# A long convolution by Fourier transforms in front of a feed-forward layer: the transform over s2 split by halves instead of parities

## The chip, the core and the metric

The kernel runs on one core of a Trainium2 chip. The metric is the device time of one execution in microseconds. A ratio is the mean time of one kernel's runs over the mean of the kernel before's runs of the same rounds. A kernel counts as faster or slower only beyond 2%.

A few words that the text uses. A *stage* is a stretch of the execution with one kind of work. A *group* is the work on one pair of frequencies k1, of which there are 45 for each of the four batches. The *period* of batch 0's groups is the length of their stage divided by 44. The *tail* is the stretch after the last group's filter product in which the remaining steps of batch 0 run out, before the feed-forward layer starts.

## The reference

```python
def _attn_ref(x, v, pos_emb, w1, w2):          # x, v: (4, 12544, 128)
    h_mlp = np.maximum(pos_emb @ w1, 0.0) @ w2
    h_filt = h_mlp * np.exp(-0.01 * pos)[:, None]
    u = x * v
    Uf = np.fft.rfft(u, n=2 * S, axis=1)
    Hf = np.fft.rfft(h_filt, n=2 * S, axis=0)
    y = np.fft.irfft(Uf * Hf[None], n=2 * S, axis=1)[:, :S, :]
    return x * y

def _moe_ref(x, w1, w2, w3, w_out):            # x: (50176, 128), d_ff 768
    h = np.maximum(np.maximum(x @ w1, x @ w2), x @ w3)
    return h @ w_out
# output: _moe_ref(_attn_ref(...).reshape(50176, 128), ...)
```

The kernel makes the convolution from matmuls with tables of sines and cosines. A position is n*128 + s2. The first transform runs over n and leaves, for every s2, 90 frequencies k1. The second runs over s2 and leaves the frequencies k2. Then comes the product with the filter's transform. The third transform goes back to s2 and the last one back to n.

## The kernel before

The 128-point transform over s2 is never done whole. Before the change it is split by the parity r of s2: each parity is transformed alone, and the sum and difference of the two results (a butterfly) give the lower and the upper half of k2. After the product, another sum and difference (`g_unfold`, whose result is `ab`) prepares the two inputs of the third transform. The cuts from the code leave out lines that only name or rearrange views (`v`, `xt`, `d0` and the like); other gaps are marked with three dots.

```python
def first_halves(ps, lhs, table, dst, copy):        # first transform, then one copy
    for i, a in enumerate(lhs):
        for r in range(2):
            for c in range(2):
                nc.tensor.matmul(ps[64 * c:64 * c + 64, 256 * i + r * N1:256 * i + (r + 1) * N1],
                                 a[:, r, :], table[:, c * N1:(c + 1) * N1], ...)
    copy(dst, ps[:].rearrange("p (s m) -> p s m", m=256)[:, :, 0:2 * N1].rearrange(
        "p s (r k) -> p k r s", r=2))

def evens(ps, eo):                                  # ScalarE
    nc.scalar.copy(eo[:], v[:, :, 1, :])
def butterfly(ps, eo, xs):                          # VectorE, from PSUM
    nc.vector.tensor_tensor(out=xs[:, :, 0, :], in0=eo[:], in1=v[:, :, 0, :], op=ALU.add)
    nc.vector.tensor_tensor(out=xs[:, :, 1, :], in0=eo[:], in1=v[:, :, 0, :], op=ALU.subtract)
def g_re(g):                                        # product: both inputs in SBUF
    nc.vector.tensor_tensor(out=xt[:], in0=xt[:], in1=hts[g][:, 0], op=ALU.mult)
def g_im(g):
    nc.vector.tensor_tensor(out=xss[g][:], in0=xss[g][:], in1=hts.pop(g)[:, 1], op=ALU.mult)
def g_sum(g, eng):
    eng.tensor_tensor(out=xts[g][:], in0=xts[g][:], in1=xss.pop(g)[:], op=ALU.add)
def g_unfold(g):                                    # both inputs in SBUF
    for q, op in enumerate((ALU.add, ALU.subtract)):
        nc.vector.tensor_tensor(out=ab[:, :, q, :], in0=y[:, :, 0, :], in1=y[:, :, 1, :], op=op)
def g_third(b, g): ...                              # third transform of ab
def g_pair(g):                                      # batches 1 to 3: from PSUM
    nc.vector.tensor_tensor(out=zs[:, a], in0=ps[:, 0:256], in1=z1[:], op=op)

# ... beside the feed-forward layer: the slots of one group (a slot is some 2.9 us)
            at(s, 1, g_second, g)
            at(s + 1, 0, g_butterfly, g)
            at(s + 2, 1, g_swap, g)
            at(s + 3, 0, g_re, g)
            at(s + 4, 0, g_im, g)
            at(s + 5, 0, g_sum, g, nc.gpsimd)
            at(s + 7, 0, g_unfold, g)
            at(s + 8, 1, g_third, b, g)
            at(s + 9, 0, g_pair, g)
            at(s + 10, 0, g_store, b, g, nc.gpsimd)

# ... one hidden block of the feed-forward layer
        halves_mm(pa[:, 0:N], w_sb[1][:, f * P:(f + 1) * P], rhs, True, True)
        nc.scalar.activation(h[:], pa[:, 0:N], Relu)
        halves_mm(pb[:, 0:N], w_sb[2][:, f * P:(f + 1) * P], rhs, True, True)
        nc.vector.tensor_tensor(out=h[:], in0=h[:], in1=pb[:, 0:N], op=ALU.max)
```

Batch 0 is transformed alone, before the feed-forward layer starts; batches 1 to 3 are transformed beside the feed-forward layer of the batch before them.

## Time and profile before

The median of four runs is 2479.1 us (2478.58 to 2484.12). I cut the profiled execution at five events: the data's first transform, the first and the last product that makes the filter (`sps`), and the first matmul of the last transform (`yps`), where the feed-forward layer starts.

| stage of the kernel before | from, us | to, us | length, us |
|---|---|---|---|
| set-up, filter's network and first transforms | 0 | 67.1 | 67.1 |
| first transforms of batch 0 | 67.1 | 127.1 | 60.0 |
| 45 groups of batch 0, a period of 4.02 us | 127.1 | 303.8 | 176.7 |
| tail | 303.8 | 320.4 | 16.6 |
| four feed-forward stages | 320.4 | 2480.6 | 2160.2 |

The view by windows of the kernel before shows four of these stages. The columns are window, length, busy us of PE, PEld, DVE, ACT and POOL with their instructions, granted clock, DMA share and GB/s.

```profile
67.10:127.10 60.00, 59.09 (x1190) 54.70 (x1188) 30.97 (x73) 40.39 (x50) 1.54 (x2) 1.00 0.74 173
127.10:303.80 176.70, 175.82 (x2458) 146.13 (x2456) 155.05 (x313) 151.96 (x268) 46.23 (x88) 1.00 0.88 267
320.40:897.50 577.10, 547.29 (x6344) 378.57 (x6346) 395.34 (x739) 222.87 (x454) 354.21 (x390) 0.99 0.75 177
897.50:1474.80 577.30, 545.61 (x6628) 371.77 (x6626) 425.12 (x761) 230.06 (x468) 370.42 (x411) 0.99 0.78 183
```

Take the first row. TensorE is busy for 59.09 of 60 us, and GpSimd does nothing (1.54 us): the first transforms are bound by TensorE. In the second row TensorE has 175.82 of 176.7. The two feed-forward rows leave 30 and 32 us of TensorE idle each. That idle time is what the change wants.

### The profile page before, as it was taken

How to read it: one execution, taken by the hardware profiler on the slowest of the kernel's cores; microseconds unless marked ns; L12 is line 12 of the kernel's file. 1: busy time of each engine (PE TensorE's matmuls, PEld its weight loads, DVE VectorE, ACT ScalarE, POOL GpSimd, SP SyncE). 2: the span in 40 equal slices, each digit the busy share in tenths (PEclk: the TensorE clock that was granted, in tenths of full speed). 3: DMA queues.
4: the chain of work that ended last, by engine and by line, in shares of the span. 5: the costliest groups of instructions: out<-in, count | busy, mean ns of one | idle time of the engine just before them, and what ended most of it. 6: DMA issues, size and time to landing. Idle time of an engine off the chain costs nothing.

```text
span 2480.6 us, 70451 instructions
## 1 busy us (share of the span) xinstructions
PE 2373.3 (96%) x29025; PEld 1655.7 (67%) x29025; DVE 1628.5 (66%) x3044; ACT 1008.8 (41%) x1981; POOL 1395.9 (56%) x1595
## 2 busy tenths in 40 slices
PE   9999999999999899999999999998999999999999
PEld 8988867766666656666666666765666666666665
DVE  4588847577777756667888856758878873333333
ACT  2688834444334324434434433443444432222222
POOL 1022247566656567646666667656666665555565
PEclk9999999999999999999999999999999999999999
DMA  6879889777677649958778749967787843222231
GB/s 147 193 237 275 265 163 187 144 189 213 170 197 203 156 112 200 183 132 215 201 200 212 208 120 176 189 149 197 193 214 193 216 125 90 51 67 60 54 73 21
DMA packets 459275, 408.67 MB, mean 165 GB/s; under 512 B 322660, under 2 KB 338333, under 8 KB 458953
## 3 DMA queue, kind: packets, MB, share of 16 engines
q1 hardware_dynamic: 417664, 315.23, 54.2%
q0 software_dynamic: 28464, 75.72, 11.1%
q10 hardware_dynamic: 12825, 13.21, 1.7%
q8 instruction: 228, 3.74, 0.6%
q14 instruction: 94, 0.77, 0.1%
HBM read 295.76 MB, written 84.67 MB: 153 GB/s over the span
## 4 chain that ended last, share of the span: by engine, by line
PE 81%; DVE 11%; DMA 4%; issue 2%; ACT 1%; SPq 0%; ACTq 0%; POOL 0%; DVEq 0%; POOLq 0%
PE pb L131 17%; PE pa L131 17%; PE ops L624 17%; PE ps L131 12%; PE ps L140 7%; PE yps L131 5%; DVE ab L444 4%; PE sps L798 3%; DMA ht<-hd 3%; DVE hid L578 2%; DVE zs L470 1%; DVE xs L434 1%; PE pm L304 1%; PE gps L784 1%; DVE xt L431 1%
## 5 line engine op out<-in xcount | busy, mean ns | idle before, releaser
L578 DVE TENSOR_TENSOR hid<-hid,pb 128x392 f32<-128x392 f32 x768 | 429.1, 559 | 506.6 <-PE pb L131 439.6
L575 ACT ACTIVATE hid<-pa 128x392 f32<-128x392 f32 x768 | 382.3, 498 | 709.3 <-PE pa L131 682.7
L131 PE MATMUL pa<-gt,w_sb 128*64 128x392 f32 x3072 | 641.0, 495 | 0.0
L131 PE MATMUL pb<-gt,w_sb 128*64 128x392 f32 x3072 | 638.6, 494 | 0.6 <-ACT hid L575 0.6
L131 PEld LDWEIGHTS pb<-gt,w_sb 128*64 128x64 f32 x3072 | 221.2, 137 | 288.8 <-issue 271.6
L624 PE MATMUL ops<-hid,wo_sb 128*64 128x196 f32 x3072 | 330.9, 329 | 0.0
L624 PEld LDWEIGHTS ops<-hid,wo_sb 128*64 128x64 f32 x3072 | 220.6, 137 | 138.3 <-issue 113.0
L649 POOL DMA_DIRECT2D out_dram<-o x256 | 162.7, 640 | 264.4 <-DVE o L644 104.8
L131 PE MATMUL ps<-ab,wt 128*64 128x128 f32 x2880 | 205.5, 281 | 87.2 <-DVE ab L444 84.4
L594 POOL TENSOR_TENSOR s<-hid 128x392 f32<-128x392 f32 x192 | 205.2, 1069 | 134.0 <-DVE hid L578 130.9
L594 POOL TENSOR_TENSOR s<-hid,s 128x392 f32<-128x392 f32 x192 | 200.7, 1045 | 97.7 <-DVE hid L578 96.8
L444 DVE TENSOR_TENSOR ab<-xt 128x256 f32<-128x256 f32 x360 | 252.5, 741 | 1.6
L131 PEld LDWEIGHTS ps<-ab,wt 128*64 128x64 f32 x2880 | 162.1, 138 | 130.8 <-DVE ab L444 110.6
L594 POOL TENSOR_TENSOR hid<-hid,s 128x392 f32<-128x392 f32 x192 | 206.4, 1081 | 42.6 <-DVE hid L578 24.4
L437 POOL TENSOR_TENSOR xt<-xt,xs 128x512 f32<-128x512 f32 x135 | 172.4, 1277 | 96.5 <-DVE xs L434 81.6
L131 PEld LDWEIGHTS pa<-gt,w_sb 128*64 128x64 f32 x3072 | 200.7, 138 | 20.1 <-issue 2.2
L431 DVE TENSOR_TENSOR xt<-xt,ht 128x512 f32<-128x512 f32 x180 | 203.0, 1128 | 13.9 <-ACT ht L803 13.7
L594 POOL TENSOR_TENSOR hid<-hid 128x392 f32<-128x392 f32 x192 | 209.8, 1111 | 0.2
L131 PE MATMUL ps<-spec,wt 128*64 128x128 f32 x2880 | 189.2, 273 | 2.1 <-issue 2.1
L140 PE MATMUL ps<-f,uT 98*64 98x90 f32 x4096 | 188.1, 241 | 2.4 <-ACT spec L144 2.3
L140 PEld LDWEIGHTS ps<-f,uT 98*64 98x64 f32 x4096 | 176.4, 137 | 12.2 <-ACT spec L144 5.5
L624 PE MATMUL ops<-s,tw 128*64 128x196 f32 x1536 | 171.3, 329 | 0.0
(105 smaller groups left out, 3083.4 us busy)
## 6 DMA issues: line engine op xcount, KB each, us to landing
wt<-wt_const SPq DMA_DIRECT2D x360, 256.0 KB, 4.7
ht<-hd SPq DMA_DIRECT2D x270, 256.0 KB, 4.4
zd<-zs POOLq DMA_DIRECT2D x135, 256.0 KB, 3.6
zt<-zd SPq DMA_DIRECT2D x192, 180.0 KB, 4.3
ut<-in_xr_dram SPq DMA_DIRECT2D x128, 196.0 KB, 4.1
ut<-in_vr_dram SPq DMA_DIRECT2D x128, 196.0 KB, 4.2
xT<-in_x_dram SPq DMA_DIRECT2D x256, 98.0 KB, 4.2
out_dram<-o POOLq DMA_DIRECT2D x256, 98.0 KB, 3.3
```

Of the source, the lines that this page charges most:

```text
L131: nc.tensor.matmul(out[64 * h:64 * h + 64], lhsT[:, 64 * h:64 * h + 64], rhs, start=start, stop=stop, skip_group_check=True)
L140: nc.tensor.matmul(ps[64 * c:64 * c + 64, 256 * i + r * N1:256 * i + (r + 1) * N1], a[:, r, :], table[:, c * N1:(c + 1) * N1], start=(i % ...
L304: nc.tensor.matmul(ps[64 * h:64 * h + HH, 512 * r + q * FO:512 * r + (q + 1) * FO], posv[64 * h:64 * h + 64, P - 1 - 2 * (8 * i + q) - r, ...
L431: nc.vector.tensor_tensor(out=xt[:], in0=xt[:], in1=hts[g][:, 0], op=ALU.mult)
L437: eng.tensor_tensor(out=xts[g][:], in0=xts[g][:], in1=xss.pop(g)[:], op=ALU.add)
L444: nc.vector.tensor_tensor(out=ab[:, :, q, :], in0=y[:, :, 0, :], in1=y[:, :, 1, :], op=op)
L575: nc.scalar.activation(h[:], pa[:, 0:N], Relu)
L578: nc.vector.tensor_tensor(out=h[:], in0=h[:], in1=pb[:, 0:N], op=ALU.max)
L594: nc.gpsimd.tensor_tensor(out=out[:], in0=a[:], in1=b[:], op=op)
L624: nc.tensor.matmul(ps[64 * c:64 * c + 64, 0:H2], w, rhs[:, :, c, :], start=start, stop=True, skip_group_check=True)
L649: nc.gpsimd.dma_start(dst[64 * m:64 * m + 64, 4 * i + c:4 * i + 8:2, b, :], t[m][64 * c:64 * c + 64].rearrange("d k (q n) -> d (k q) n", q=2))
L798: nc.tensor.matmul(ps[64 * h:64 * h + 64, (2 * c + k) * 2 * D:(2 * c + k + 1) * 2 * D], G[:, k, c], w2x[:].rearrange("p s d -> p (s d)"), ...
```

## The change

The transform over s2 is split by the halves w of s2 instead. The two halves are summed and subtracted straight after the first transform, while they lie in first-stage PSUM (`over_w`); each result is then transformed to one parity c of k2. There is no butterfly after the second transform, so the product can read the second transform from PSUM, and no sum stands between the product and the third transform. On the way back the two parities are summed out of third-stage PSUM (`g_over_c`), one half is turned by a quarter (`g_turn`), and `g_pair` joins the two k1. In batch 0, some of the new half-sums go to GpSimd (`over_w_there`, `filter_over_w`). The filter's product becomes 32 matmuls of 64 rows in quarters of the array, in place of 16 of 128 rows. Batch 0's last transform takes the half-size table that the other batches already had.

```diff
+    def over_w(ps, dst, tmp):
+        v = by_r(ps)                                # "p (s m) -> p s r k"
+        nc.scalar.copy(tmp, v[:, :, 1, :])
+        for c, op in enumerate((ALU.add, ALU.subtract)):
+            nc.vector.tensor_tensor(out=dst[:, :, c, :].rearrange("p k s -> p s k"), in0=tmp,
+                                    in1=v[:, :, 0, :], op=op)
+    def over_w_there(ps, dst, tmp):
+        nc.scalar.copy(tmp, v[:, :, 1, :])
+        nc.scalar.copy(d0, v[:, :, 0, :])
+        nc.gpsimd.tensor_tensor(out=d1, in0=tmp, in1=d0, op=ALU.subtract)
+        nc.gpsimd.tensor_tensor(out=d0, in0=tmp, in1=d0, op=ALU.add)
+    def as_it_is(ps, dst):
+        nc.scalar.copy(dst.rearrange("p k r s -> p s r k"), by_r(ps))
...
     def g_re(g):
-        nc.vector.tensor_tensor(out=xt[:], in0=xt[:], in1=hts[g][:, 0], op=ALU.mult)
+        nc.vector.tensor_tensor(out=xt[...], in0=ps[:], in1=hts[g][:, 0]..., op=ALU.mult)
-    def g_unfold(g): ...
+    def g_over_c(g):                                # VectorE, from PSUM
+        dt = state["cv"][0].tile([P, 5, D], FP32, tag="dt", name="dt", bufs=1)
+        for w, op in enumerate((ALU.add, ALU.subtract)):
+            nc.vector.tensor_tensor(out=dt[...], in0=c0, in1=c1[:], op=op)
+    def g_turn(g):                                  # ScalarE
+        nc.scalar.copy(dt[0:64, 3, :], dt[64:128, 4, :])
+        nc.scalar.mul(dt[64:128, 3, :], dt[0:64, 4, :], -1.0)
     def g_pair(g):                                  # now both inputs in SBUF, all batches
-            nc.vector.tensor_tensor(out=zs[:, a], in0=ps[:, 0:256], in1=z1[:], op=op)
+            nc.vector.tensor_tensor(out=zs[:, a], in0=dt[:, 0:2, :], in1=dt[:, 2:4, :], op=op)
...
+            at(s + 1, 0, g_swap, g)
+            at(s + 1, 0, g_re, g)
+            at(s + 2, 0, g_im, g)
+            at(s + 3, 0, g_sum, g)
+            at(s + 5, 1, g_third, g)
+            at(s + 6, 0, g_over_c, g)
+            at(s + 6, 1, g_turn, g)
+            at(s + 7, 1, g_pair, g)
+            at(s + 9, 0, g_store, b, g)
...
+    def filter_over_w(k):                           # the filter's half-sums, five k at a time
+        nc.gpsimd.tensor_tensor(out=t, in0=s1, in1=s0, op=ALU.subtract)
+        nc.gpsimd.tensor_tensor(out=s0, in0=s1, in1=s0, op=ALU.add)
+        nc.scalar.copy(s1, t)
...
             quad([t[:, 4 * v + i] for i in range(4)], f1[:], spec[:, :, :, at:at + 4],
+                 over_w_there if (u + v) % 5 in (1, 3) else over_w)
+            if at < 4 * N1 // 5:
+                filter_over_w(5 * at // 4)
...
+    for s in range(-1, NK + 5):                     # batch 0's groups
+        s_filter(s); g_second(s); g_swap(s); g_re(s)
+        s_second(s + 1)
+        g_turn(s - 3)
+        g_third(s - 2)
+        g_im(s); g_sum(s)
+        g_pair(s - 3)
+        g_over_c(s - 2)
+        g_store(0, s - 4)
...
-                        G[:, k, c], w2x[:].rearrange("p s d -> p (s d)"), start=(k == 0),
+                            G[64 * c:64 * c + 64, k, ri, :], w2x[64 * c:64 * c + 64],
```

The loop over batch 0's groups is shown without its conditions on s, and its weight loads are left out.

## The prediction

> **What bounds the kernel now.** I read the page's busy times and chain first, to see which engine carries the time.
>
> ```profile
> PE 2373.3 (96%) x29025; PEld 1655.7 (67%) x29025; DVE 1628.5 (66%) x3044; ACT 1008.8 (41%) x1981; POOL 1395.9 (56%) x1595
> ...
> PE 81%; DVE 11%; DMA 4%; issue 2%; ACT 1%; SPq 0%; ACTq 0%; POOL 0%; DVEq 0%; POOLq 0%
> ```
>
> TensorE is busy for 96%, but 11% of the chain is VectorE. So the bulk is matmul time that this change leaves alone, and the prize is in the stretches where VectorE ends the wait. I then cut the span into stages with the view by windows. Set-up and first transforms run to 124 us; batch 0's middle transform with the filter (45 groups) to 304; then four feed-forward stages, the first three of which carry the next batch's transform: inputs and first transform first, then 45 groups of second transform, product and third transform. Four of the windows inside the feed-forward stages:
>
> ```profile
> 506.00:885.00 379.00, 351.30 (x3953) 241.94 (x3950) 280.55 (x535) 148.58 (x309) 237.83 (x248) 0.99 0.69 180
> 910.00:1080.00 170.00, 168.13 (x2312) 116.57 (x2310) 108.29 (x189) 69.18 (x133) 114.73 (x144) 1.00 0.97 179
> 1085.00:1460.00 375.00, 345.18 (x3994) 234.59 (x3992) 303.77 (x544) 151.60 (x316) 238.84 (x248) 0.99 0.71 188
> ...
> 1660.00:2035.00 375.00, 345.48 (x3998) 235.00 (x3995) 303.45 (x548) 152.44 (x317) 238.78 (x248) 0.99 0.71 189
> ```
>
> Columns: window, length, busy us of PE, PEld, DVE, ACT, POOL, clock, DMA share, GB/s. Where first transforms are made (910 to 1080) TensorE idles 2 us of 170. Where the groups run it idles 28, 30 and 30 us, 87 in all, with VectorE 74 to 81% busy. The waits from 325 to 2030 us say for what:
>
> ```profile
> PEld ps L131 <- DVE ab L444: 105.6, 73, 4.9
> ...
> PE ps L131 <- DVE ab L444: 83.9, 64, 4.6
> ```
>
> `ab` is the sum and difference of the product, made by VectorE just before the third transform. 64 waits, 84 us: practically all of the idle time. Why VectorE is late shows in the groups of lines of 1085 to 1460 us:
>
> ```profile
> L444 DVE TENSOR_TENSOR ab<-xt 128x256 f32<-128x256 f32 x90 | 76.2, 885 | 0.0
> ...
> L431 DVE TENSOR_TENSOR xt<-xt,ht 128x512 f32<-128x512 f32 x45 | 61.4, 1365 | 0.0
> L434 DVE TENSOR_TENSOR xs<-xs,ht 128x512 f32<-128x512 f32 x45 | 34.7, 771 | 0.0
> L470 DVE TENSOR_TENSOR zs<-ps,z 128x256 f32<-128x256 f32 x88 | 32.9, 415 | 0.0
> ```
>
> The same forms in 124 to 304 us, where GpSimd only issues transfers:
>
> ```profile
> L444 DVE TENSOR_TENSOR ab<-xt 128x256 f32<-128x256 f32 x86 | 32.7, 422 | 1.5
> ...
> L431 DVE TENSOR_TENSOR xt<-xt,ht 128x512 f32<-128x512 f32 x44 | 30.4, 691 | 13.6 <-ACT ht L803 13.3
> ```
>
> 885 against 422 ns, 1365 against 691 ns: beside GpSimd's arithmetic, the operations with both inputs in SBUF take twice their time. The one with an input in PSUM (`zs`) stays at 415.
>
> **What the skill says.** The Trainium skill, "SBUF — State Buffer", section "SBUF: two separate sides": GpSimd and a VectorE operation with two SBUF inputs take a shared port pair as an exclusive lock for a whole instruction. The trace agrees (the pairs above; the longest `ab` took 4.86 us). "PSUM — Partial Sum Buffer", "The four PSUM rules": GpSimd cannot touch PSUM; so whatever this change reads from PSUM it must leave to VectorE or ScalarE. "TensorEngine Tiling (Array Packing)", "Key Properties": 64x64 tiles work independently, and changing the tiling mode drains the array. No quarter-array products of the new form are in this trace. "TensorE: Matmul & The Clock Gate", "Wait — 56ns, not 53.3ns?": start-to-start does not drop below about 25 ns however short the matmul. The trace agrees: 32 matmuls of 49 columns (`yps` from `f4p`) start at 2100.16 and their successor at 2101.08, 0.92 us, 29 ns each.
>
> **The change part by part.**
>
> (a) *Groups beside the feed-forward layer, 3 x 45.* VectorE now does, in one group: butterfly 2 x 0.41, product 1.365, second product 0.77, `ab` 2 x 0.885, final pair 2 x 0.415 = 5.6 us. After: the first product reads PSUM (0.69, taken from its undisturbed time, since it has one SBUF input); second product 0.77; sums over c from PSUM 2 x 0.415; the final pair, now with both inputs in SBUF, 2 x 0.65 (between 0.42 free and 0.885 blocked) = 3.6 us. 2 us less of some 8.3 us a group. More than the load, the order counts: nothing of VectorE stands any more between GpSimd's sum and the third transform, and the lengthened final pair is behind the matmuls. The sum is made in slot 3, the third transform comes late in slot 5; a slot is some 2.9 us, the sum takes 1.28. Before, `ab` came two slots after that sum too and idled only 1.6 us before starting, so the sum is in time by two slots. I expect 25 to 30 us of the 87 us of idle time to stay, from PSUM buffers held while VectorE lags: gain 60.
>
> (b) *First transforms beside the feed-forward layer.* Each half: instead of one copy (482 or 525 ns) one ScalarE copy of half the size and two VectorE operations of 180 columns from PSUM (0.34 each, from 351 ns at 196 columns). The joining copy moves from VectorE (1047 ns, blocked) to ScalarE (770). Per input VectorE goes 2.25 to 2.05 us, ScalarE 1.25 to 2.1 of 5.3. TensorE is already at 168 of 170 us there: 0.
>
> (c) *Last transform of batch 0* takes the half-size table: 32 calls whose 32 matmuls go from 1.36 us (98 columns, start 364.20 to 365.56) to 0.92. TensorE bounds there: 32 x 0.44 = 14 us gained.
>
> (d) *Batch 0's groups, 45 of 3.96 us.* Here TensorE and ScalarE are both full. One period of the timeline:
>
> ```profile
> 164.25 1.10 PE L131 MATMUL ps<-ab,wt 128*64 128x128 f32 x16
> ...
> 165.18 0.60 PE L784 MATMUL gps<-wt,specH 128*64 128x128 f32 x8
> ...
> 165.61 1.04 PE L131 MATMUL ps<-spec,wt 128*64 128x128 f32 x16
> ...
> 166.49 1.90 PE L798 MATMUL sps<-w2x,G 128*64 128x256 f32 x16
> ...
> 168.21 1.04 PE L131 MATMUL ps<-ab,wt 128*64 128x128 f32 x16
> ```
>
> Start to start: 0.93 + 0.43 + 0.88 + 1.72. The filter's product (1.72) becomes 32 matmuls of 128 columns with half the rows; a pair of 128 columns now takes 0.11, so eight sets of four are 0.88, the issue floor 32 x 29 ns = 0.92, plus two mode changes: about 1.05. TensorE would go to 3.3 us. ScalarE, from its starts: filter copy 0.92, two swaps 1.3, G 0.35, c1 0.4, two turns of 128 columns 0.55 (266 ns for a 128x128 copy) = 3.5; the half-sums copy 0.38, the 0.59 result copy and a transfer issue of 0.37 go. DMA is at 0.82 of 3.96 = 3.2. VectorE 0.69 + 0.69 + 0.83 + 0.76 = 3.0; GpSimd gets the sum (1.28) and the store (0.72) beside two filter stores (1.06) = 3.1. So ScalarE would bound at 3.5, a gain of 45 x 0.45 = 20. But the sum on GpSimd now runs directly beside the final pair, which may wait up to 1.28 us for it: VectorE at 4.2, and nothing gained. I take 12.
>
> (e) *Batch 0's first transforms, 32 quads of 1.82 us.* VectorE, GpSimd and ScalarE now share sums that one ScalarE copy (760 ns) did not need. GpSimd: 13 quads x 2 x 0.95 (360 columns, from 1.02 at 392) and 18 filter sums x 2 x 0.87 (320 columns), 56 us, of which 45 fall in the first 18 quads that take 33 us now; ScalarE's copy back waits for them. Loss 8 (0 to 20).
>
> Sum: -60 - 14 - 12 + 8 = -78; 2479 - 78 = 2401, so 2400.
>
> **Rivals.** *The wait only changes its name*: the third transform waits for GpSimd's sum or for PSUM, as the new order has fewer slots (5 instead of 8 from second to third transform). For it: GpSimd is 64% busy in those windows; c1 and the turned sums have one buffer each, and a turn on ScalarE can hold up the next relu. Against: the slack computed in (a). It would leave only (c) and (d): about 2455. *GpSimd's lock becomes the bound in batch 0's stages*: (d) gives 0 and (e) costs 20; 2425. *Everything works*: all 87 us of idle gone, (d) at 20, (e) at 0: 2360. *A transfer hides it*: loads at 0.97 share in first transforms are not touched, and in the groups the share is 0.7; little speaks for it.
>
> **Range and chances.** The sum lies between 2360 and 2455; the middle eighty per cent 2364 to 2440. The 2% limit is 2430; only the first rival reaches it. Faster 0.83, same 0.14, slower 0.03.
>
> **What would show it.** (a): in the group windows TensorE's idle falls under 10 us each and no wait of the third transform over 20 us in total; the first product's mean is near 700 ns; the final pair's mean is well over 415. (c): 49-column `yps` in batch 0, that stage shorter by 14 us more than the other two. (d): filter products 1.05 us start to start, a period near 3.6 with ScalarE full. (e): quads of over 1.82 us with ScalarE waiting for GpSimd. It is wrong if third transforms wait for `xt`, or relu for turns, by tens of us.

## The result, and the profile after

The kernel after takes 2510.41 us (median of four runs, 2503.55 to 2513.47) against 2479.1 us. The ratio is 1.0118 (95% interval 1.0092 to 1.0144): 1.2% slower, which is within 2%. The prediction of 2400 us (2364 to 2440) and "faster" at 0.83 were wrong. All outputs are right.

The same five cuts in the profiled execution of the kernel after give this account. The execution profiled was the fastest of the four, with a span of 2501.8 us.

| stage | before, us | after, us | difference, us | predicted, us |
|---|---|---|---|---|
| to the data's first transform | 67.1 | 67.6 | +0.5 | 0 |
| first transforms of batch 0 | 60.0 | 114.4 | +54.4 | +8 |
| 45 groups of batch 0 | 176.7 (period 4.02) | 196.4 (period 4.46) | +19.7 | -12 |
| tail | 16.6 | 29.5 | +12.9 | not in the sum |
| four feed-forward stages | 2160.2 | 2093.9 | -66.3 | -74 |
| sum | 2480.6 | 2501.8 | +21.2 | -78 |

So the last two thousand microseconds behaved as predicted, and the first 400 did not. The windows of the kernel after, with the same columns as above:

```profile
67.60:182.00 114.40, 76.46 (x1148) 67.72 (x1144) 73.50 (x119) 45.28 (x80) 69.66 (x68) 0.78 0.37 90
182.00:378.40 196.40, 158.15 (x3181) 137.94 (x3184) 136.29 (x256) 152.21 (x304) 129.20 (x170) 0.97 0.77 234
378.40:407.90 29.50, 20.28 (x308) 16.99 (x301) 19.96 (x52) 12.22 (x36) 8.12 (x10) 0.88 0.39 114
407.90:961.20 553.30, 529.23 (x6344) 360.97 (x6346) 365.98 (x698) 248.47 (x551) 347.36 (x390) 0.99 0.75 184
961.20:1516.40 555.20, 538.14 (x6628) 373.12 (x6626) 392.63 (x735) 260.49 (x577) 361.99 (x411) 1.00 0.81 191
```

The first row is the one to learn from. In 114.4 us TensorE is busy 76.46, VectorE 73.50, GpSimd 69.66 and ScalarE 45.28 us, and the transfers use 0.37 of their engines. Nothing is near its limit, so the time goes to engines waiting for one another in turn. TensorE's clock has fallen to 0.78, so even its busy time is longer than the 59.09 us of before. In the second row TensorE's busy time has fallen from 175.82 to 158.15 us, because the filter's product is cheaper, yet the stage is longer. In the two feed-forward rows TensorE's idle time is 24 and 17 us, from 30 and 32.

The page's busy times, its chain of what ended last, and its slices in 40ths of the span agree with this:

```profile
PE 2344.5 (94%) x29745; PEld 1651.8 (66%) x29745; DVE 1562.3 (62%) x2969; ACT 1109.3 (44%) x2371; POOL 1528.2 (61%) x1746
PE   8678877999999999999999999999999999999998
PEclk9779998999999999999999999999999999999999
PE 73%; DVE 7%; ACT 4%; DMA 4%; issue 3%; POOL 0%; SPq 0%; DVEq 0%; ACTq 0%; POOLq 0%
```

But for the last slice, only the first seven of TensorE are below 9. VectorE's part of the chain has fallen from 11% to 7%, which is the wait that the change set out to remove; ScalarE's has risen from 1% to 4%.

Of the groups of lines in the two middle feed-forward stages (960 to 2071.5 us), these answer to those shown in the prediction. The numbers at the end are busy us, mean ns of one, and idle time just before with its releaser.

```profile
L131 PE MATMUL ps<-xt,wt 128*64 128x128 f32 x1440 | 94.5, 273 | 1.4 <-issue 1.4
L432 DVE TENSOR_TENSOR xt<-ps,ht 128x512 f32<-128x512 f32 x90 | 61.5, 683 | 17.4 <-POOL s L587 7.6 <-ACT xs L426 5.9 <-issue 2.1
L471 DVE TENSOR_TENSOR zs<-dt 128x256 f32<-128x256 f32 x180 | 162.7, 943 | 0.0
L131 PE MATMUL pb<-gt,w_sb 128*64 128x392 f32 x1540 | 320.4, 493 | 18.5 <-ACT hid L568 18.5
```

The third transform (`ps` from `xt`) waits 1.4 us in all, where it waited tens of microseconds for `ab`. The first product takes 683 ns instead of 1365, because one of its inputs is now in PSUM. The final pair has gone the other way, from 415 to 943 ns. The fourth line is a new wait: the matmul of the second weight (`pb`) waits 18.5 us in these two stages for ScalarE's relu.

In the first transforms the view of waits (71 to 150 us) names the cycle. Its columns are time waited, times, and the longest.

```profile
ACT specH L712 <- POOL specH L711: 47.6, 18, 5.3
DVE spec L154 <- ACT tmp L152: 33.8, 7, 6.8
PE pst L357 <- DVE ut L352: 27.0, 9, 5.4
```

The timeline shows one turn of it (start, length, work, and in brackets the idle time before and what ended it; here and in the timelines below, lines of other work are left out):

```profile
84.58 1.21 POOL L164 TENSOR_TENSOR spec<-tmp,spec 128x360 f32<-128x360 f32 x1
85.73 0.86 POOL L710 TENSOR_TENSOR misc<-specH 128x320 f32<-128x320 f32 x1
86.67 0.86 POOL L711 TENSOR_TENSOR specH<-specH 128x320 f32<-128x320 f32 x1
87.56 0.46 ACT L712 COPY specH<-misc 128x320 f32<-128x320 f32 x1 [4.68 <-POOL specH L711]
88.83 0.46 ACT L152 COPY tmp<-ps 128x360 f32<-128x360 f32 x1
89.32 1.40 DVE L154 TENSOR_TENSOR spec<-tmp,ps 128x360 f32<-128x360 f32 x2 [5.90 <-ACT tmp L152]
91.46 1.22 DVE L352 TENSOR_TENSOR ut<-ut 128x392 f32<-128x392 f32 x1
92.74 1.09 PE L357 MATMUL pst<-eye,ut 128*98 128x128 f32 x4 [4.29 <-DVE ut L352]
93.76 4.58 PE L140 MATMUL ps<-f,uT 98*64 98x90 f32 x64
```

ScalarE stands for 4.68 us on a copy of the filter's half-sum, which needs GpSimd. Behind that copy in ScalarE's queue is the copy `tmp` of the next quad, which needs nothing from GpSimd. VectorE stands 5.90 us for `tmp`. Behind its half-sums is the product `ut` of the inputs, which needs neither. TensorE stands 4.29 us for the transpose of that product. Then its 64 matmuls take 4.58 us; after an idle time of only 1.31 us the same 64 took 2.70 us (at 72.68 us). Each engine waits for its neighbour at the front of its queue, with work behind that needs no such wait.

### The profile page after: what moved, and what is told of

Its sections match the earlier page's. It is cut to its first block, busy times and chain, and to the rows that moved or that the text cites. A ratio compares the mean times of both kernels' runs of the same rounds, so it can differ in the third digit from the quotient of the medians.

```text
span 2501.8 us, 73325 instructions
## 1 busy us (share of the span) xinstructions
PE 2344.5 (94%) x29745; PEld 1651.8 (66%) x29745; DVE 1562.3 (62%) x2969; ACT 1109.3 (44%) x2371; POOL 1528.2 (61%) x1746
## 4 chain that ended last, share of the span: by engine, by line
PE 73%; DVE 7%; ACT 4%; DMA 4%; issue 3%; POOL 0%; SPq 0%; DVEq 0%; ACTq 0%; POOLq 0%
PE ops L617 19%; PE pb L131 18%; PE pa L131 18%; PE ps L131 9%; PE ps L140 5%; PE yps L131 4%; DVE zs L471 3%; DMA zd<-zs 2%; DVE dt L456 2%; ACT hid L568 1%; DVE xs L437 1%; DMA hd<-ht 1%; ACT xs L426 1%; ACT xs L425 1%; ACT dt L464 1%
## 5 line engine op out<-in xcount | busy, mean ns | idle before, releaser
L440 POOL TENSOR_TENSOR xt<-xt,xs 128x512 f32<-128x512 f32 x180 | 234.7, 1304 | 168.4 <-DVE xs L437 129.6
L471 DVE TENSOR_TENSOR zs<-dt 128x256 f32<-128x256 f32 x360 | 290.0, 845 | 42.2 <-DMA zd<-zs 35.6
L154 DVE TENSOR_TENSOR spec<-tmp,ps 128x180 f32<-128x180 f32 (+1 forms) x422 | 172.3, 503 | 110.6 <-ACT tmp L152 110.1
L587 POOL TENSOR_TENSOR hid<-hid,s 128x392 f32<-128x392 f32 x192 | 198.7, 1039 | 43.2 <-DVE hid L571 24.1
L131 PEld LDWEIGHTS pa<-gt,w_sb 128*64 128x64 f32 x3072 | 199.3, 137 | 34.1 <-DVE hid L571 10.6
L140 PE MATMUL ps<-f,uT 98*64 98x90 f32 x4096 | 203.6, 253 | 9.7 <-DVE dt L456 4.2
L140 PEld LDWEIGHTS ps<-f,uT 98*64 98x64 f32 x4096 | 191.3, 146 | 21.6 <-issue 9.7
L587 POOL TENSOR_TENSOR hid<-hid 128x392 f32<-128x392 f32 x192 | 200.4, 1059 | 0.5
L558 DVE TENSOR_TENSOR gt<-yps,xT 128x392 f32<-128x392 f32 x128 | 72.3, 565 | 200.3 <-PE ops L617 155.1
L131 PE MATMUL ps<-xt,wt 128*64 128x128 f32 x2880 | 189.8, 274 | 3.7 <-issue 2.1
L131 PEld LDWEIGHTS ps<-spec,wt 128*64 128x64 f32 x2880 | 163.2, 138 | 16.4 <-DVE dt L456 4.6
```

What stands on the lines that cost most here:

```text
L131: nc.tensor.matmul(out[64 * h:64 * h + 64], lhsT[:, 64 * h:64 * h + 64], rhs, start=start, stop=stop, skip_group_check=True)
L154: nc.vector.tensor_tensor(out=dst[:, :, c, :].rearrange("p k s -> p s k"), in0=tmp, in1=v[:, :, 0, :], op=op)
L440: nc.gpsimd.tensor_tensor(out=xts[g][:], in0=xts[g][:], in1=xss.pop(g)[:], op=ALU.add)
L471: nc.vector.tensor_tensor(out=zs[:, a], in0=dt[:, 0:2, :], in1=dt[:, 2:4, :], op=op)
L558: nc.vector.tensor_tensor(out=g[:].rearrange("d (w t) (m a) -> d w t m a", w=2, a=2), in0=y, in1=xT.rearrange("d w t (m a) -> d w t m a", ...
L587: nc.gpsimd.tensor_tensor(out=out[:], in0=a[:], in1=b[:], op=op)
```

## The experiments

All kernels are edits of the kernel after, timed in three rounds against the kernel before. What an edit gains on the kernel after is computed from ratios: (1.0118 minus its ratio) times 2479 us. With the intervals of both ratios this is good to some 8 us, so stage lengths from the profile are given beside it. They scatter too: in the runs that leave a stage's code alone, the first transforms took 114.4 to 116.1 us, and the period of batch 0's groups was 4.36 to 4.52 us. The theories at the start, for the time lost in batch 0 and beside the feed-forward layer, were the filter's copy in ScalarE's queue, GpSimd's share of the half-sums, the order of the elements in the half-sums, and the turn in front of the relu. Later runs added the result buffers and the order of batch 0's groups.

### 1. The filter's copy one quad later

```diff
-        nc.scalar.copy(s1, t)
+        return lambda: nc.scalar.copy(s1, t)        # called after the next quad's copies
```

> Edit: the ScalarE copy that brings the filter's difference back is issued one quad later; same instructions on the same engines. Theory 1: in the changed kernel batch 0's first transforms take 110 us (67.5 to 178) instead of 53 because that copy stands in ScalarE's queue behind two to four GpSimd operations and holds up everything that ScalarE does next. Then they fall to 65-80 us here and the time goes from 2510 to about 2470-2480. Rival: GpSimd's amount of work (52 us busy of 79) or its lock on VectorE sets the pace; then the stage stays above 95 us and the time above 2495.

Measured: 2492.18 us (2486.92 to 2497.05), ratio 1.0039 (1.0019 to 1.0060), a gain of 20 us. The first transforms took 102.1 us instead of 114.4; the wait of the copy for GpSimd fell from 47.6 to 20.5 us. The copy in the queue is one cause, but most of the 54 us stayed. The expectation of 65 to 80 us for the stage was missed; the stage stayed above 95 us, as the rival (GpSimd's amount of work, or its lock on VectorE) would have it. Run 2 takes up that rival.

### 2. All of the data's half-sums on VectorE

```diff
-                 over_w_there if (u + v) % 5 in (1, 3) else over_w)
+                 over_w)
```

> Edit: all 32 quads of batch 0 take their half-sums on VectorE, none on GpSimd; the filter's sums and their copy stay as they are. Theory 1 (the filter's copy is the brake): each of the first 18 quads still waits for the filter's two sums, so only 10-20 us are gained, 2490-2500. Rival (the 13 quads on GpSimd are the brake): the first transforms fall below 75 us and the time to about 2470.

Measured: 2480.99 us (2480.45 to 2482.28), ratio 0.9995 (0.9978 to 1.0012), a gain of 30 us, between what the theory (10 to 20 us) and its rival (a stage below 75 us) expected. The stage by windows:

```profile
66.00:156.00 90.00, 67.60 (x1150) 58.80 (x1147) 84.11 (x145) 37.91 (x67) 37.08 (x42) 0.90 0.47 115
```

Now 90 us instead of 114.4, and VectorE is busy for 84.11 of them. With fewer turns of waiting the stage has found a bound: VectorE's amount of work. Taking sums off GpSimd helps even though it loads an engine that was already busy: VectorE's wait for `tmp`, 44.1 us in this stage of the kernel after, is 8.9 us here.

### 3. Four result buffers in batch 0's groups

```diff
-        zs = state["cv"][0].tile([P, 2, 2, D], FP32, tag="z", name="zs", bufs=2)
+        zs = state["cv"][0].tile([P, 2, 2, D], FP32, tag="z", name="zs", bufs=state.get("zb", 2))
...
-    state = {"cv": (cvp, cps), "turn": cps, "xb": 2, "xsb": 2}
+    state = {"cv": (cvp, cps), "turn": cps, "xb": 2, "xsb": 2, "zb": 4}    # batch 0
```

> Edit: four result buffers instead of two in batch 0's groups. Theory 2: the period of a group there is 4.46 us instead of 4.01 because the final pair on VectorE waits until the store of two groups ago, now a GpSimd transfer that is issued late, has landed. Then the wait for that store disappears, the period falls to 3.6-3.9 us and the time by 25-38 us to about 2472-2485. Rival: ScalarE or the filter's new product (33 us of waiting for the filter's first-stage copy) sets the pace; then the period stays at 4.3 or more and the time within 8 us of 2510.

It did not build: its pool needed 31.9375 kB per partition and 28.75 kB were left. Nothing was measured. Run 5 takes the same wait away in another way.

### 4. The half-sums in another element order

The half-sums in the kernel after write with k innermost: consecutive elements lie 1 KB apart. The copy of before wrote with s innermost, two or four adjacent elements at a time. This run restores that order. It does not remove the hop of 1 KB but moves it: now the reads from PSUM take it, and the writes are adjacent.

```diff
-            nc.vector.tensor_tensor(out=dst[:, :, c, :].rearrange("p k s -> p s k"), in0=tmp,
-                                    in1=v[:, :, 0, :], op=op)
+            nc.vector.tensor_tensor(out=dst[:, :, c, :], in0=tmp, in1=v[:, 0], op=op)   # p k s
```

> Edit: the half-sums and filter copies run over s innermost, so that neighbouring elements are written one after another, as in the kernel before; same count of instructions. Theory 3: VectorE's 180-column sums take 476 ns instead of the predicted 340, and the filter's copies 1516 ns instead of 760, because consecutive elements are written far apart. Then they return to about 340 and 760 ns, and the time falls by 5-15 us, mostly in the lead-in. Rival: the durations come from waiting for the shared port or for PSUM; then they stay.

Measured: 2494.92 us (2490.44 to 2501.83), ratio 1.0053 (1.0030 to 1.0076), a gain of 16 us; the first transforms took 102.2 us. The same two groups of lines, first in the kernel after, then in this run:

```profile
L154 DVE TENSOR_TENSOR spec<-tmp,ps 128x180 f32<-128x180 f32 x384 | 145.6, 476 | 66.5 <-ACT tmp L152 66.0
L167 ACT COPY specH<-ps 128x720 f32<-128x720 f32 x16 | 21.4, 1516 | 20.2 <-PE ps L140 20.2
```

```profile
L155 DVE TENSOR_TENSOR spec<-tmp,ps 128x180 f32<-128x180 f32 x384 | 112.3, 337 | 74.0 <-ACT tmp L153 73.2
L168 ACT COPY specH<-ps 128x720 f32<-128x720 f32 x16 | 12.2, 760 | 26.3 <-PE ps L140 26.3
```

VectorE's half-sum goes from 476 to 337 ns and ScalarE's copy of the filter from 1516 to 760 ns. VectorE's 360-column form went from 778 to 524 ns, and GpSimd's from about 1300 to between 1025 and 1088. The theory was confirmed in its numbers. The Trainium skill, "Vector Engine (DVE) Microarchitecture Reference", section "Measured stream behaviour on trn2", says that a port runs at full rate only while its elements come in runs of at least two adjacent words, and gives 1.71 against 1.054 ns per column where the destination hops at every element, which is 0.66 ns more. This trace shows (476 - 337)/180 = 0.77 and (778 - 524)/360 = 0.71 ns more per column. The page would have corrected my 0.34 us for the half-sums before the run, had I asked how the new operation *writes* and not only what it reads.

### 5. The store one group earlier

In batch 0's loop the store of a group's result is issued one turn of the loop after the pair that makes it, behind GpSimd's other work, and there are two buffers.

```diff
             g_pair(s - 3)
+            g_store(0, s - 3)
...
-            g_store(0, s - 4)
```

> Edit: in batch 0's groups the store of a result is issued directly behind the final pair that makes it, one group earlier than in the changed kernel; no buffer is added (four result buffers did not fit). Theory 2 (the final pair waits for the late store of two groups ago to land, and that sets the 4.46 us a group): the wait of the final pair for the store vanishes, the period falls to 3.6-4.0 us, the time by 20-38 us to 2472-2490. Rival: ScalarE or the filter's first-stage copy, for which the filter's product waits 33 us, sets the period; then it stays at 4.3 or more and the time within 8 us of 2510.

Measured: 2486.66 us (2486.22 to 2492.05), ratio 1.0035 (1.0020 to 1.0050), a gain of 21 us. The group's period fell from 4.46 to 4.22 us. The wait for the store is in the line of the final pair, after and here:

```profile
L471 DVE TENSOR_TENSOR zs<-dt 128x256 f32<-128x256 f32 x360 | 290.0, 845 | 42.2 <-DMA zd<-zs 35.6 <-ACT xs L426 4.5 <-ACT ht L813 2.0
```

```profile
L471 DVE TENSOR_TENSOR zs<-dt 128x256 f32<-128x256 f32 x360 | 305.3, 888 | 0.5 <-ACT dt L464 0.3 <-DMA zd<-zs 0.2
```

The wait of 35.6 us for landed stores went to 0.2, but the mean of the pair rose from 845 to 888 ns. The timeline of this run shows why:

```profile
253.59 1.84 DVE L471 TENSOR_TENSOR zs<-dt 128x256 f32<-128x256 f32 x2
253.85 1.29 POOL L440 TENSOR_TENSOR xt<-xt,xs 128x512 f32<-128x512 f32 x1 [0.44 <-ACT c L447]
```

The pair, freed of its wait, now lands beside GpSimd's sum and takes 1.84 us; without a sum beside it two such operations took 0.75 us (run 9). That is the shared port that the prediction's part (d) had as its risk. The period fell between what the theory and its rival expected.

### 6. Runs 2 and 4 together

> Edit: the two earlier ones together, all data half-sums on VectorE and s innermost. Theory 3 and what the run with all sums on VectorE showed: its 64 sums fall from 786 to about 525 ns, so VectorE, which was 94 per cent busy there, has 17 us less to do; the first transforms fall from 88 to 70-76 us and the time from 2481 to 2460-2470. Rival: the filter's sums on GpSimd, whose copy ScalarE waits for, now set the pace; then they stay above 82 us and the time above 2474.

Measured: 2469.53 us (2467.94 to 2471.54), ratio 0.9962 (0.9947 to 0.9976), a gain of 39 us. The first transforms took 83.8 us; 70 to 76 had been expected. The gains of single edits do not add: 30 and 16 gave 39. VectorE was busy for 74.96 of the 83.8 us, so it is near its limit there, which would explain it. The rival, the filter's sums on GpSimd, had the stage above 82 us, which came true, and the time above 2474 us, which did not; run 8 takes it up.

### 7. The turn half a slot later

```diff
-            at(s + 6, 1, g_turn, g)
-            at(s + 7, 1, g_pair, g)
-            at(s + 9, 0, g_store, b, g)
+            at(s + 7, 0, g_turn, g)
+            at(s + 8, 0, g_pair, g)
+            at(s + 10, 0, g_store, b, g)
```

> Edit: in the feed-forward stages the turn (two ScalarE copies that need VectorE's sums over c), the final pair and the store move to the next slots, 7, 8 and 10. Theory 4: the 43 us that TensorE still idles there (32 before pb for the relu, 11 before pa for the maximum) come from turns that stand in ScalarE's queue ahead of the relu and wait for VectorE (261 us of waiting in all). Then the idle time before pb falls under 12 us and the time by 15-30 us to 2480-2495. Rival: the relu is late because VectorE's maximum keeps the hidden buffers; then the wait before pb stays above 25 us and the time within 8 us of 2510.

In the kernel after, the timeline shows a relu behind a turn:

```profile
1194.33 2.64 DVE L471 TENSOR_TENSOR zs<-dt 128x256 f32<-128x256 f32 x2
1196.34 0.83 PE L131 MATMUL pa<-gt,w_sb 128*64 128x392 f32 x4
1198.11 0.74 DVE L456 TENSOR_TENSOR dt<-ps,c 128x256 f32<-128x256 f32 x2
1198.94 0.30 ACT L463 COPY dt<-dt 64x128 f32<-64x128 f32 x1 [5.02 <-DVE dt L456]
1199.58 0.50 ACT L568 ACTIVATE hid<-pa 128x392 f32<-128x392 f32 x1
1200.13 0.88 PE L131 MATMUL pb<-gt,w_sb 128*64 128x392 f32 x4 [0.64 <-ACT hid L568]
```

The matmul `pa` of 1196.34 is done by about 1197.2, but its relu starts at 1199.58. ScalarE stood in front of the turn, which needed VectorE's sum `dt` at 1198.11, which stood behind a pair of 2.64 us. TensorE then waits for the relu.

Measured: 2476.72 us (2474.78 to 2480.05), ratio 0.9992 (0.9977 to 1.0006), a gain of 31 us; 15 to 30 had been expected. From the first `yps` to the end it took 2066.8 us, against 2093.9 in the kernel after. Over the whole run, the line of `pb` after and here:

```profile
L131 PE MATMUL pb<-gt,w_sb 128*64 128x392 f32 x3072 | 639.9, 494 | 32.5 <-ACT hid L568 32.3
```

```profile
L131 PE MATMUL pb<-gt,w_sb 128*64 128x392 f32 x3072 | 639.2, 493 | 3.3 <-ACT hid L568 3.0
```

The wait is gone, and with it that of `pa`, from 11.0 to 1.9 us.

### 8. No half-sums on GpSimd

Run 6, and the filter's half-sums on VectorE straight from PSUM, like the data's:

```diff
         quad([hs[:, f + i] for i in range(4)], f1h[:], specH[:, :, :, f:f + 4],
-             as_it_is)
+             over_w)
...
-            if at < 4 * N1 // 5:
-                filter_over_w(5 * at // 4)
```

> Edit: as the one before (VectorE, s innermost), and the filter's half-sums too are made by VectorE as each filter quad comes out of PSUM, so GpSimd adds nothing before the groups. Theory 1: without any filter sum to wait for, the data's first transforms fall to 58-68 us; the filter's own quads gain 16 x 2 x 0.52 = 17 us of VectorE work and may stretch from 23 to 28-40 us; time 2455-2470. Rival: VectorE's whole work (86 us in the 81 us that the two parts took in the kernel before) bounds; then both parts together take over 105 us and the time is above 2475.

Measured: 2469.66 us (2465.95 to 2473.06), ratio 0.9958 (0.9941 to 0.9975). The data's first transforms took 77.1 us, but they began 5.8 us later than in run 6 (72.1 against 66.3 us), since the filter's sums come earlier. The total equals run 6. From 45 to 150 us VectorE was busy 94.4 of 105 us. That fits the rival, by which VectorE's work bounds both stages together wherever the sums stand, but the time above 2475 us that it asked for did not come.

### 9. The pair moved in front of the sum

An attempt to keep the pair away from GpSimd's sum: the turn and the pair of group s-3 come before the second product of group s, with the early store of run 5.

```diff
             s_filter(s)
+            g_turn(s - 3)
             g_second(s)
             g_swap(s)
             g_re(s)
+            g_pair(s - 3)
+            g_store(0, s - 3)
             s_second(s + 1)
-            g_turn(s - 3)
```

> Edit: batch 0's groups with the store directly behind the final pair, and the final pair of three groups ago moved in front of the second product (its turn between the filter's copy and the swaps), so that GpSimd's sum runs beside operations that read PSUM. Theory 5: with the store early the period was 4.22 us with VectorE 92 per cent busy, because the final pair (1.84 us instead of 0.8) is locked out by GpSimd's sum that starts with it. Then the pair falls to about 0.8 us, the period to 3.6-3.9 us, the time by 15-25 us more than with the early store alone, to 2462-2472. Rival: ScalarE (85 per cent busy) or the transfers (0.83 share) set the period; then the pair gets shorter but the period stays above 4.1 and the time above 2480.

Measured: 2509.44 us (2506.58 to 2513.50), ratio 1.0122 (1.0107 to 1.0137): nothing gained on the kernel after, and 22 us lost against run 5. The pair did become short (0.75 us for two), but the period rose to 4.68 us, and 38 of the 44 intervals between groups are 4.62 or 4.63 us. The timeline shows a loop:

```profile
254.00 0.59 ACT L425 ACTIVATE xs<-ps 64x512 f32<-64x512 f32 x1
255.21 0.37 ACT L795 COPY G<-gps 128x256 f32<-128x256 f32 x1
255.63 1.10 PE L808 MATMUL sps<-w2x,G 64*64 64x128 f32 x32 [1.19 <-ACT G L795]
256.81 1.01 ACT L813 COPY ht<-sps 128x1024 f32<-128x1024 f32 x1 [0.95 <-PE sps L808]
```

The swaps (`xs`), the copy `G`, TensorE's filter product and the copy `ht` follow one another, and ScalarE is in the loop three times. TensorE waits 1.19 us for ScalarE, then ScalarE 0.95 us for TensorE. This miss was useful: the period was set by a loop through ScalarE's queue, not only by the shared port.

### 10 and 11. Run 6 or run 8, with every repair known by then

Both take the order of run 9 and the turn of run 7, and make both input products of a pair of quads before their half-sums. Run 10 builds on run 6 with the deferred copy of run 1, and run 11 on run 8.

> All repairs together: data half-sums on VectorE with s innermost, the filter's sums on GpSimd with ScalarE's copy a quad later, both input products of a round issued before its sums, the group order of the run before, the turn in the next slot. If the gains are in separate stages they add: about 40 + 42 + 34 us off 2510, 2385-2400, 3 to 4 per cent faster than the kernel before. If they share a bound (TensorE's own order in the feed-forward stages would not see the lead-in), less than half of the later ones remains and the time is above 2420.

> As the run before, but the filter's half-sums on VectorE too and no arithmetic of GpSimd before the groups. VectorE was 90 per cent busy there, so I expect the same time within 6 us (2385-2402); more than 10 us slower would mean that VectorE's amount of work, not the order, bounds the lead-in; more than 6 us faster that the lock of GpSimd's filter sums still costs.

Measured: 2446.49 us (2446.03 to 2447.60), ratio 0.9868 (0.9852 to 0.9885), and 2443.53 us (2443.24 to 2447.38), ratio 0.9859 (0.9844 to 0.9874). Both beat the kernel before by over 1%, and they differ little, as expected. Run 10 missed its 2385 to 2400, for the larger part because both carry the order of run 9: their periods were 4.67 and 4.66 us, and run 14, which is run 11 with another order and the sum of run 13, is some 29 us faster by the ratios. In run 11 the first transforms took 72.1 us against 77.1 in run 8; of its edits only the order of the input products touches that stage. This order was not run by itself.

### 12. The copy G in front of the swaps

```diff
             s_filter(s)
+            s_second(s + 1)             # with its ScalarE copy G, ahead of the swaps
             g_second(s)
             g_swap(s)
             g_re(s)
-            s_second(s + 1)
```

with the early store of run 5.

> Edit against the changed kernel: the early store, and the filter's first-stage product and its ScalarE copy issued in front of the data's second transform and swaps, so that the copy stands directly behind the previous filter copy in ScalarE's queue. Theory 6: a group's period is set by a loop through ScalarE's in-order queue: filter copy, swaps, first-stage copy, then TensorE's filter product, then the next filter copy (the run with the pair moved put the turn into that loop as well and went to 4.68 us). Then TensorE's wait of the filter product for the first-stage copy (28 us with the early store alone) goes under 5 us. The final pair is still locked out by GpSimd's sum, so VectorE, 92 per cent busy of 4.22, holds the period at 3.9-4.1 and the time at 2475-2484. Rival (the transfers, share 0.83 with the early store): the wait for the copy moves to transfers and the period stays at 4.2, 2486.

Measured: 2488.64 us (2484.56 to 2493.90), ratio 1.0029 (1.0013 to 1.0045), a gain of 22 us. The period averaged 4.12 us against run 5's 4.22. In an undisturbed stretch it is 3.80 us, read from the starts of the second product in this run:

```profile
253.72 0.68 DVE L437 TENSOR_TENSOR xs<-xs,ht 128x512 f32<-128x512 f32 x1
...
257.52 0.68 DVE L437 TENSOR_TENSOR xs<-xs,ht 128x512 f32<-128x512 f32 x1
```

The same reading gives most often 4.12 us in the kernel after and 3.86 to 3.95 us in run 5. TensorE's wait for `G` fell from 28.4 us in run 5 to 17.6, where under 5 had been expected. So the loop through ScalarE was part of the period, a small one in this order; the difference of the means, 0.10 us, lies within their scatter. The time as a whole does not differ from run 5's beyond their spread, and the expected 2475 to 2484 was missed.

### 13. Run 12 with batch 0's sum on VectorE

```diff
-            g_sum(s)                    # GpSimd
+            g_sum(s, nc.vector)
```

> As the run before, and batch 0's sum of the two products goes back to VectorE, where it was before the change, so no arithmetic of GpSimd meets VectorE's two-SBUF operations there. Theory 5 (the lock of that sum costs): VectorE has 3.66 us of work a group, ScalarE 3.5, TensorE 3.3; the pair falls to 0.8 us, the period to 3.7-3.85, time 2464-2474. Rival (lock does not matter once the copy is early): no faster than the run before within 5 us, or slower for the 0.69 us that VectorE takes over.

Measured: 2485.98 us (2483.36 to 2489.01), ratio 1.0017 (1.0003 to 1.0032). The pair went from 1.83 to 0.75 us, but the period only from 4.12 to 4.03 and the time by some 3 us, within the spread. The expected 3.70 to 3.85 was missed. But the mean hides that undisturbed groups became faster. The starts of the second product, with the view of waits from 200 to 340 us:

```profile
250.18 0.68 DVE L437 TENSOR_TENSOR xs<-xs,ht 128x512 f32<-128x512 f32 x1
...
253.63 0.68 DVE L437 TENSOR_TENSOR xs<-xs,ht 128x512 f32<-128x512 f32 x1
```

```profile
ACT ht L813 <- DMA hd<-ht: 10.8, 11, 1.6
```

That is 3.45 us, where run 12 had 3.80. Of the 25 intervals between the starts of ScalarE's swaps from 200 to 300 us, 16 are 3.43 to 3.68 us long. The other nine, 4.06 to 5.48 us, are just those in which the copy `ht` had to wait, by the trace in seven of them for the landed store of an earlier `ht`, of which there are two buffers. So the long pair had not been in the slack: without GpSimd's sum an undisturbed group takes 0.35 us less, and the intervals with a wait for filter stores take it back (in run 12 there are eight of them, 3.82 to 4.77 us long). The edit frees GpSimd's queue as well as the shared port, so it does not tell the two apart, and no run had more buffers for `ht` or fewer transfers.

### 14. The repairs together

Run 8 with both input products first, the turn of run 7, the early store of run 5, the copy of run 12 and the sum of run 13.

> All repairs, with this group order in place of the one that failed: filter and data half-sums on VectorE with s innermost, both input products of a round first, turn in the next slot, early store, early first-stage copy, batch 0's sum on VectorE. The same with the failed group order took 2443.5 with a period of 4.66 us; at 3.75 us the 45 groups give back 41 us: 2400-2410, about 3 per cent faster than the kernel before.

Measured: 2417.90 us (2414.62 to 2421.18), ratio 0.9741 (0.9724 to 0.9757). It is 2.6% faster than the kernel before and some 93 us faster than the kernel after. The expected 2400 to 2410 was missed by 8 us, as the period was 4.05 us. Its stages (first transforms, groups, tail, feed-forward), with the columns as above:

```profile
73.20:144.10 70.90, 59.01 (x1144) 53.48 (x1144) 68.39 (x164) 30.19 (x49) 4.74 (x9) 0.98 0.61 149
144.10:322.10 178.00, 155.57 (x3182) 136.64 (x3184) 144.41 (x297) 147.93 (x302) 74.80 (x127) 0.98 0.82 258
322.10:350.00 27.90, 20.04 (x306) 16.84 (x299) 19.62 (x55) 12.95 (x38) 5.71 (x9) 0.88 0.41 122
350.00:2417.50 2067.50, 2027.37 (x23840) 1381.97 (x23840) 1344.19 (x2476) 877.77 (x1931) 1307.53 (x1474) 1.00 0.68 164
```

VectorE is busy for 68.39 of 70.9 us in the first transforms, so that stage is now bound by work. The clock is back at 0.98. Against the kernel before, the lead-in still costs 350.0 - 320.4 = 29.6 us, and the feed-forward part gains 2160.2 - 2067.5 = 92.7 us.

## Why the prediction was wrong, point by point

The prediction missed the profiled span by 99 us (+21.2 against -78). By stages that is 46 us in the first transforms, 32 in batch 0's groups, 13 in the tail, 8 in the feed-forward part and 0.5 before.

**(a), the groups beside the feed-forward layer: right in mechanism, and near in size.** The wait on `ab` left, the first product took 683 ns (690 predicted), and the pair went "well over 415". The two stages where nothing else changed are 22 us shorter each. What the prediction kept as 25 to 30 us of remaining idle time "from PSUM buffers held" was larger and of another kind: 43 us over the whole run in which the feed-forward layer's own matmuls waited (32 of `pb` for relus, 11 of `pa` for VectorE's maxima). Rival one had named it ("a turn on ScalarE can hold up the next relu"), and the prediction's own sign of being wrong, "relu for turns, by tens of us", came true; run 7 shows it, by taking 27 us off the feed-forward part with later slots alone.

**(b), first transforms beside the feed-forward layer: zero, as said**, although the half-sum took 476 ns and not 340. There TensorE bounds, and the misjudged duration was hidden: run 4 brought the half-sum to 337 ns, and its feed-forward part took 2096.0 us against 2093.9.

**(c), 14 us in batch 0's last transform: the matmuls fell, the stage less so.** TensorE's busy time fell by 18.1 us in that feed-forward stage, where the other two lost 7.5 each: 10.6 us more, for the 14 expected. But the stage became shorter by 23.8 us, only some 2 more than the others, since more of its TensorE time is idle (24 against 17 us). That the later start of batch 1's inputs causes this was not tested. It is partly luck, then, that the feed-forward part came near to its 74 us: (a), at some 22 us a stage, gave 66 of the measured 66.3, and (c) some 2, about what the last stage lost (1.3 us).

**(d), batch 0's groups: wrong in sign.** The step that failed is "So ScalarE would bound at 3.5", with "I take 12". The size of the filter's product was right: 1.04 us from its start to that of the next matmuls (252.78 to 253.82) for a predicted 1.05. But adding up each engine's busy time gives the least period that the engines allow, and I took it for the period that the order allows. Two chains that my sum did not hold set it: the result's store, issued late on GpSimd's queue, with two buffers (run 5: 4.46 to 4.22 us), and the loop from the swaps through `G` and the filter's product to `ht` on ScalarE (run 9 lengthened the period to 4.68; with run 12 undisturbed groups took 3.80 us). The lock of the pair by GpSimd's sum, which I had as the risk, is real in the trace (1.84 us against 0.75). With the sum on VectorE undisturbed groups take 3.45 us (run 13), so the 3.5 of my sum can be reached, but only with all three repairs; the mean stays at 4.03 us, with waits of `ht` for landed filter stores, which my sum did not hold either.

**(e), batch 0's first transforms: the step that cost the most.** The step that failed is "GpSimd: ... 56 us, of which 45 fall in the first 18 quads that take 33 us now; ScalarE's copy back waits for them. Loss 8 (0 to 20)". Even its own figures ask for more: 45 us of GpSimd work in a stretch of 33 us make a loss of 12 if all goes well. The runs showed +54.4 us, in three kinds:

- Waits in queues that run in order. ScalarE's copy waited 47.6 us for GpSimd, and everything behind it waited too. A copy one quad later shortened the stage by 12 us (run 1); the data's sums on VectorE alone, which removes the slowest partner from the cycle, by 24 us (run 2).
- Durations. With elements 1 KB apart the 360-column half-sum took 778 ns, not the 521 to 524 of the adjacent order; that order shortened the stage by 12 us (run 4).
- The clock. The cycle leaves TensorE idle for up to 5.4 us at a time (27.0 us in nine waits), and its clock was 0.73 from 71 to 150 us. The Trainium skill, "TensorE: Matmul & The Clock Gate", section "What's actually happening", says that an idle window of about 3.4 us puts the array back to half speed. The trace agrees: after an idle time of 4.29 us and a short transpose, 64 matmuls took 4.58 us instead of 2.70, 1.7 times as long. No run isolates what this adds. In run 14 it is gone together with the waits.

These overlap and do not add: single edits shortened the stage by 12, 24 and 12 us, and runs 2 and 4 together by 31 (114.4 to 83.8). How the 54 us divide among the three is left open. What is shown is that VectorE's own work is the floor afterwards (68.39 of 70.9 us in run 14), and that this floor lies 11 us above the old stage.

**The tail: not in the prediction at all.** It grew by 12.9 us. By the timeline, the last group goes through more steps (third transform, sums, turn, pair, store), each in its own turn of the loop, with a wait of up to 1.36 us for a landed store, and the half-sums of batch 1's first inputs follow. TensorE waits there for the sums `dt` 1.56, 2.35 and 1.86 us, and from 388.9 to 391.6 us its clock was 0.50, although none of these gaps is as long as those of the first transforms. The tail was still 27.9 us in run 14. No run tested it, so this reading is only argued.

**The rivals.** Of the four, "GpSimd's lock becomes the bound in batch 0's stages" pointed to the right place, but at 20 us for (e) it was far too small, and the runs show waits in queues and durations before the lock. The lock is there too: from 66 to 144 us the product `ut` took 833 ns in the kernel after and 560 ns in run 8, which has no sums on GpSimd. What that adds to the 54 us was not isolated. "The wait only changes its name" held for part of the feed-forward stages. The chance of "slower" or "same" was put too low: only one rival had batch 0's stages slower than the sum, and by 24 us in all.

Left open: what would bring batch 0's groups, which still average 4.05 us in run 14, to the 3.45 us of an undisturbed stretch. The waits left are spread over TensorE for `G` (20.1 us), ScalarE for landed filter stores (14.4 us) and the early inputs of batch 1, with the transfers at a share of 0.82. At 3.45 us the same transfers would need some 0.96 (an estimate, 0.82 x 4.05 / 3.45), so they are the rival that no run tested.

## What to carry to other kernels

A sum of busy times per engine is a lower bound, not a forecast: where a change lets three engines hand each tile to one another, write down the order of each queue and ask what stands behind the instruction that waits. Moving work from a copy to sums also changes how it writes, so check the distance between consecutive output elements before you take a duration from another line. And when a change pays in the long stages and costs in the short ones, look at the short ones for order rather than for amount: here four changes of order in queues, an order of elements and sums moved to VectorE turned 1.2% slower into 2.6% faster.

## What the Trainium skill lacked or had wrong

- "ScalarE: Activation LUTs" has nothing on the order of output elements. ScalarE's copy of 128x720 from PSUM took 1516 ns with k innermost and 760 ns with four adjacent elements innermost, 1.05 ns more per column, which is more than VectorE pays (0.71 to 0.77). "SBUF — State Buffer" has a penalty for accesses that cross to a new cache line, but no figure for it.
- "TensorEngine Tiling (Array Packing)", "Key Properties", says that a change of tiling mode drains the array, but gives no duration. 32 matmuls of 128 columns in quarter arrays took 1.04 us start to start with a change on either side; the prediction's issue floor for 32 matmuls (0.92 us, measured at 49 columns) leaves some 0.12 us for both changes, an estimate.
- "Vector Engine (DVE) Microarchitecture Reference", "Measured stream behaviour on trn2", has 0.66 ns more per column for a destination that hops 4 KiB at every element. It has neither a hop of 1 KB nor one on a read from PSUM: with the hop on the write instead of on that read, run 4 shows 0.71 to 0.77 ns more per column (524 ns against 778 for 360 columns).
